# First bias rows copied inside SBUF, and the head of an attention and adapter kernel dealt out anew

## The chip, the cores and the metric

The kernel runs on one core of one Trainium2 chip. The metric is the device time of one execution in microseconds (us). Engines are named PE (matmuls), VectorE or DVE, ScalarE or ACT (exponentials and copies), POOL or GpSimd, and SP, which only issues DMAs here.

## The reference

Attention with eight heads and eight batches over 576 positions of 64 elements, with a bias that depends on the distance of query and key alone, followed by a mixture of low-rank adapters (top two of eight experts) on the joined heads.

```python
scores = scale * np.matmul(q, k.transpose(0, 1, 3, 2))
n = np.abs(pos[:, None] - pos[None, :])
bucket = np.where(n < half, n, large)        # 32 buckets, constant from distance 128 on
scores = scores + bias_table[bucket].transpose(2, 0, 1)[None]
attn = softmax(scores)
x = (attn @ v) joined over heads             # 4608 x 512
logits = x @ w_gate                          # top 2 of 8, softmax over the two
out = x + sum over the two of w * ((x @ A[e]) @ B[e])
```

## The kernel before

Work is cut into 32 units: a unit is a batch `b` and a pair of heads `hp` (four pairs to a batch), so unit u is pair u % 4 of batch u // 4; the text calls units 0 to 5 pairs 0 to 5. In a unit the first 512 positions form the main part, `keys(u, c)` for four key tiles c in the order `KO = (0, 2, 1, 3)`: PE multiplies keys by queries (L434), adds the bias by matmuls of the table `Wt` with a reversed identity `anti` (L439), and ACT takes the exponential into `pk` (L443). The last 64 positions are the tail: `edges(u)` has its scores against the main part (L493, L496, exponential L498 into `pt`), the corners have tail against tail (L470, exponentials L477 or L384 into `pcx`). In edges and corners the bias enters as a factor on the exponentials: `EL`, `ET` and `EC`, applied by `edge_l` (POOL), `edge_t` (DVE) and `corners_bias` (POOL). `step(u, j)` makes half of the unit's values on PE (`values`, L522 to L541) and DVE normalises them.

All orders are written out by hand, and each engine runs its instructions in that order. Queries and keys are loaded in float32 (`load`), cast to bfloat16 (`cast`, `cast_half`), and turned by PE transposes and one DVE copy (`turn`). There are three score tiles in PSUM, taken in rotation by scores and transposes, and two banks named "mm" for values, factors and fillers. `keep_busy` issues filler matmuls. Eight semaphores serve the DMAs in rotation, and a DMA waits until the one before it on its semaphore has landed.

The bias of a head depends on 128 distances. The bias table `btT` (heads in partitions) is spread into a row per head, `gp` (L182 to L196). A row is written to DRAM (`g_d`, L663), and from there `table(h)` reads 64 shifted copies of it, one for each partition, into `Wt` (L208, two DMAs of 224.5 KB, one for each head of the pairs, all four pairs at once). `near_rows` (L204) takes exponentials of parts of `Wt` into `Wn`; `factors_l` (L218) and `factors_t` (L238) turn these on PE and DVE copies them out of PSUM into `EL`, `EC`, `ET`.

Before the loop over u = 2 to 29 stands the head: loads in SP's order, casts dealt to ACT, DVE and POOL, edges of units 0, 1 and 2, corners of batch 0, near rows, the main tiles of units 0 and 1 and one of unit 2, and the two value steps of unit 0. In the loop, a unit's keys stand around the value steps of the unit before.

## Time and profile before

| what | value |
|---|---|
| time, median of 3 runs (lowest, highest) | 193.86 us (193.13, 194.42) |
| the profiled execution's own time | 195.05 us |
| its span | 193.3 us |
| PE busy | 172.6 us (89%) |
| ACT busy | 164.1 us (85%) |
| DVE busy | 136.1 us (70%) |
| POOL busy | 110.5 us (57%) |
| read from and written to HBM | 29.31 MB and 9.45 MB |

The span goes from the first to the last instruction of the profiled execution; its own time has what lies around it too. Busy times are sums over an engine's instructions; a busy matmul is not PE at its peak. A row of groups gives a line, an engine, output and input with shapes, the count, then busy time and mean, then the idle time of the engine just before and what ended it. Times in the text are us from the start of the span.

### The profile page before, as it was taken

What the parts mean: (1) busy time and instruction counts of PE and PEld (TensorE: products, weight loads), DVE (VectorE), ACT (ScalarE), POOL (GpSimd) and SP (SyncE); (2) the same over time, 40 slices, a digit from 0 to 9 for tenths busy, and PEclk for the clock granted to TensorE, in tenths of its full rate; (3) what the DMA queues carried; (4) which work ended last, traced back from release to release, by engine and by line L of the source; (5) the groups of instructions that cost most, each with busy time, mean ns of one, the idle gap of its engine ahead of it and who ended that gap; (6) DMA issues with size and microseconds to landing.
All of it is one profiled execution on the core that took longest, in us unless ns stands there. A gap on an engine that the chain in (4) does not pass through costs nothing.

```text
span 193.3 us, 9928 instructions
## 1 busy us (share of the span) xinstructions
PE 172.6 (89%) x4277; PEld 129.4 (67%) x4299; DVE 136.1 (70%) x345; ACT 164.1 (85%) x199; POOL 110.5 (57%) x249
## 2 busy tenths in 40 slices
...
ACT  3359969999999999999999989999999889898660
...
GB/s 141 241 208 282 237 266 236 215 230 227 197 215 196 222 213 214 206 254 233 249 186 238 213 189 203 257 230 247 216 256 259 197 93 111 83 138 63 3 267 221
DMA packets 63667, 39.40 MB, mean 204 GB/s; under 512 B 17408, under 2 KB 58888, under 8 KB 63624
## 3 DMA queue, kind: packets, MB, share of 16 engines
...
q14 instruction: 10, 0.08, 0.2%
HBM read 29.31 MB, written 9.45 MB: 201 GB/s over the span
## 4 chain that ended last, share of the span: by engine, by line
PE 40%; ACT 33%; issue 10%; DVE 8%; DMA 4%; SPq 0%; ACTq 0%; DVEq 0%
ACT pk L443 26%; PE pv L522 10%; PE tx L379 9%; ACT pt L498 5%; PE sc L496 3%; DMA Wt<-g_d 3%; PE sc L493 3%; PE sc L434 2%; DVE tx L381 2%; PE pv L539 2%; PE pv L530 2%; DMA g_d<-gp 2%; DVE qn L139 1%; PE sc L439 1%; ACT pk L463 1%
## 5 line engine op out<-in xcount | busy, mean ns | idle before, releaser
L443 ACT ACTIVATE pk<-sc 128x1024 bf16<-128x1024 f32 x120 | 113.0, 1037 | 2.4 <-PE sc L439 2.4
L434 PE MATMUL sc<-tx 64*64 64x512 bf16 x480 | 48.2, 384 | 0.2 <-ACT pk L443 0.2
L522 PE MATMUL pv<-v,pk 128*128 128x65 bf16 x992 | 41.4, 193 | 2.9 <-PE sc L439 2.7
L381 DVE COPY tx<-tx 128x2048 bf16<-128x2048 bf16 (+8 forms) x35 | 35.2, 1007 | 11.9 <-PE tx L379 10.0
L439 PE MATMUL sc<-Wt,anti 64*64 64x256 bf16 (+1 forms) x480 | 41.7, 306 | 1.4 <-DMA Wt<-g_d 1.4
L522 PEld LDWEIGHTS <-pk 128*128 128x128 bf16 x1024 | 37.4, 97 | 7.1 <-issue 1.9
L498 ACT ACTIVATE pt<-sc 128x1024 bf16<-128x1024 f32 x32 | 32.8, 1025 | 9.7 <-PE sc L496 7.8
L562 DVE TENSOR_TENSOR xn<-pv,rc 128x320 bf16<-128x320 f32 x62 | 30.5, 492 | 2.1
L503 POOL TENSOR_TENSOR pt<-pt,EL 128x128 bf16<-128x128 bf16 x32 | 13.7, 429 | 31.3 <-ACT pt L498 13.9
L434 PEld LDWEIGHTS <-tx 64*64 64x64 bf16 x480 | 16.9, 105 | 9.9 <-issue 0.7
L561 DVE RECIPROCAL rc<-pv 128x5 f32<-128x5 f32 x62 | 11.9, 191 | 16.1 <-PE pv L569 13.3
L304 DVE TENSOR_TENSOR ot<-dl,xn 128x512 f32<-128x512 f32 x24 | 16.6, 690 | 9.2 <-PE sc L439 6.3
L135 POOL CAST v<-vs 128x512 bf16<-128x512 f32 x32 | 19.8, 621 | 4.0 <-PE pv L541 4.0
L439 PEld LDWEIGHTS <-anti 64*64 64x64 bf16 x480 | 18.2, 105 | 1.9 <-issue 1.7
L139 POOL CAST qn<-qs 128x512 bf16<-128x512 f32 x29 | 18.4, 633 | 0.2 <-DMA qs<-in_q_dram 0.2
L139 POOL CAST kn<-ks 128x512 bf16<-128x512 f32 x29 | 18.0, 620 | 0.0
L539 PE MATMUL pv<-v,pt 128*128 128x65 bf16 x248 | 17.8, 194 | 0.0
L530 PE MATMUL pv<-vb,pt 128*128 128x130 bf16 x124 | 17.4, 223 | 0.0
L379 PEld LDWEIGHTS <-qn 64*128 64x128 bf16 x256 | 7.4, 95 | 13.6 <-issue 5.9
L482 POOL TENSOR_TENSOR pc<-pcx,EC 128x256 bf16<-128x256 bf16 x8 | 5.5, 685 | 18.2 <-ACT pcx L384 15.6
L379 PE MATMUL tx<-ident,qn 64*128 64x64 bf16 x256 | 9.4, 192 | 5.3 <-DVE qn L139 2.8
L539 PEld LDWEIGHTS <-pt 128*128 128x128 bf16 x256 | 14.0, 98 | 0.1
...
## 6 DMA issues: line engine op xcount, KB each, us to landing
...
vs<-in_v_dram SPq DMA_DIRECT2D x64, 128.0 KB, 3.6
ks<-in_k_dram SPq DMA_DIRECT2D x62, 128.0 KB, 4.2
...
vt<-in_v_dram SPq DMA_DIRECT2D x8, 128.0 KB, 4.4
qkt<-in_q_dram SPq DMA_DIRECT2D x7, 128.0 KB, 4.6
qkt<-in_k_dram SPq DMA_DIRECT2D x7, 128.0 KB, 4.8
out_dram<-ot SPq DMA_DIRECT2D x7, 128.0 KB, 2.4
```

The lines of the kernel that those rows point to most:

```text
L135: eng.tensor_copy(t[:, :, :, :D].rearrange("p c h d -> p h c d"), s)
L139: copy(t.rearrange("p c h d -> p h c d"), s)
L379: nc.tensor.transpose(ps[:, a, cols], src(i, a), ident[rows, rows])
L381: copy(sb[:, :n], ps.rearrange("p a (c i) -> p c a i", i=64)[:, :n])
L434: nc.tensor.matmul(sc[prt, h, :], lhsT=kT[rows, c * 128 + f * 64:c * 128 + f * 64 + 64], rhs=qT[rows, :], start=True, stop=False, skip_gro ...
L439: nc.tensor.matmul(_ap(sc[prt, h, :], p0, [[256, 2], [128, 2], [1, n]]), lhsT=turned(h), rhs=_ap(Wt[rows, hp, :], 2 * y0 + (GP if e else 1 ...
L443: nc.scalar.activation(probs[u][0][:, c, :, :], sc, ACT.Exp, scale=scale)
L498: nc.scalar.activation(probs[u][1][:, 64:], sc.rearrange("p h x -> p (h x)"), ACT.Exp, scale=scale)
L522: nc.tensor.matmul(pv[:, o:o + W1], lhsT=pk_slice(u, c, h, j + 2 * f), rhs=vm[:, c, h, :], start=first, stop=False, skip_group_check=True)
L530: nc.tensor.matmul(_ap(pv, h * W1, [[130, 2], [1, W1]]), lhsT=probs[u][1][:, x0:x0 + 128], rhs=tvs[b % 2][:, 2 * hp + h].rearrange("p f d ...
L539: nc.tensor.matmul(pv[:, o:o + W1], lhsT=probs[u][1][:, x0:x0 + 128], rhs=vts[u % NV][:, c, h, :], start=False, stop=False, skip_group_che ...
L562: nc.vector.tensor_tensor(xs[b][:, j, hp], _ap(pv, 0, [[W1, 5], [1, D]]), _ap(rc, 6 * j, [[1, 5], [0, D]]), op=ALU.mult)
```

## The change

The bias table is loaded by two DMAs, one on SP's and one on ACT's queue, so that the first heads of the pairs stand in partitions 0 to 3 and the second heads in 4 to 7. For pairs 0 and 1 four new DMAs on ACT's queue (`table_first`) copy the shifted rows from `gp` straight into `Wt`; `table` brings pairs 2 and 3 by way of `g_d` as before, but is issued behind `vs` and `vt` of unit 0 and `qs` and `ks` of unit 2. Near rows, left and corner factors, top factors and corners are made for pair 0 (corners: pairs 0 and 1) first and for the others later; the later top factors use a score tile and are copied out by ACT. The main tiles of unit 0 follow its edges at once; edges of unit 1 follow these; the first value step of unit 0 stands behind two key tiles of unit 1, the second one behind all four; edges of unit 2 and all its key tiles go into the loop. The casts of units 1 to 3 in the head all go to POOL. Of 24 filler matmuls 18 are left.

```diff
@@ -155,7 +155,8 @@
     GP = 256
     WN = GP + 193
     btT = cp.tile([H, NB], FP32, tag="btT")
-    nc.sync.dma_start(out=btT, in_=bias_table.rearrange("b h -> h b"))
+    for h, eng in enumerate((nc.sync, nc.scalar)):
+        eng.dma_start(out=btT[h * HP:h * HP + HP], in_=bias_table.rearrange("b (g h) -> h g b", h=2)[h])
     load(0, "k", nc.scalar)
     load(0, "q")
     load_tail(0, "qk", 0, 2)
@@ -200,13 +201,21 @@
     EC = cp.tile([128, HP * 64], BF16, tag="EC")
     Wn = cp.tile([128, 2, HP, 68], BF16, tag="Wn")
 
+    def near_one(hp):
+        nc.scalar.activation(Wn[:, :, hp].rearrange("p i (x two) -> p i x two", two=2),
+                             _ap(Wt, 128 + hp * (WN + 1), [[-64, 2], [1, 34], [GP, 2]]), ACT.Exp, scale=scale)
+
     def near_rows(i):
-        nc.scalar.activation(Wn[:, i].rearrange("p g (x two) -> p g x two", two=2),
-                             _ap(Wt, 128 - 64 * i, [[WN + 1, HP], [1, 34], [GP, 2]]), ACT.Exp, scale=scale)
+        nc.scalar.activation(Wn[:, i, 1:].rearrange("p g (x two) -> p g x two", two=2),
+                             _ap(Wt, WN + 129 - 64 * i, [[WN + 1, HP - 1], [1, 34], [GP, 2]]), ACT.Exp, scale=scale)
+
+    def table_first(hp, h, eng):
+        eng.dma_start(out=Wt[h * 64:h * 64 + 64, hp, :WN],
+                      in_=_ap(gp[h * HP + hp:h * HP + hp + 1], 0, [[1, 64], [1, WN]]))
 
     def table(h):
-        nc.sync.dma_start(out=Wt[h * 64:h * 64 + 64, :, :WN],
-                          in_=_dram(gd, 2 * h * GP, [[1, 64], [4 * GP, HP], [1, WN]]))
+        nc.sync.dma_start(out=Wt[h * 64:h * 64 + 64, 2:, :WN],
+                          in_=_dram(gd, (h * HP + 2) * 2 * GP, [[1, 64], [2 * GP, HP - 2], [1, WN]]))
 
     def table_row(rows, hp, y):
         i = 0 if y >= 256 else 1
@@ -215,37 +224,45 @@
     def turned(h):
         return anti[h * 64:h * 64 + 64, 64 - 64 * h:128 - 64 * h]
 
-    def factors_l():
-        n = HP * 64
-        ps = [mp.tile([128, 512], FP32, name="fl", tag="mm") for _ in range(2)]
-        for hp in range(HP):
+    def factor_banks(pool):
+        if pool:
+            t = pool("fl")
+            return [t[:, 0, :], t[:, 1, :]]
+        return [mp.tile([128, 512], FP32, name="fl", tag="mm") for _ in range(2)]
+
+    def factors_l(g0, g1, pool=None):
+        n = (g1 - g0) * 64
+        ps = factor_banks(pool)
+        for hp in range(g0, g1):
+            o = (hp - g0) * 64
             for e in range(2):
                 for h in range(2):
                     rows = slice(h * 64, h * 64 + 64)
                     for f in range(2):
-                        nc.tensor.matmul(ps[h][f * 64:f * 64 + 64, hp * 64 + e * 32:hp * 64 + e * 32 + 32],
+                        nc.tensor.matmul(ps[h][f * 64:f * 64 + 64, o + e * 32:o + e * 32 + 32],
                                          lhsT=table_row(rows, hp, 258 - e),
                                          rhs=_ap(turned(h), f, [[2, 32]]),
-                                         start=(hp == 0 and e == 0), stop=True, skip_group_check=True)
-                    nc.tensor.matmul(_ap(ps[h][rows], n + hp * 64 + e, [[2, 32]]),
+                                         start=(hp == g0 and e == 0), stop=True, skip_group_check=True)
+                    nc.tensor.matmul(_ap(ps[h][rows], n + o + e, [[2, 32]]),
                                      lhsT=table_row(rows, hp, 130 - e), rhs=turned(h)[:, :32],
                                      start=False, stop=True, skip_group_check=True)
         for h in range(2):
             rows = slice(h * 64, h * 64 + 64)
-            nc.vector.tensor_copy(EL[:, :, h, :], ps[h][:, :n].rearrange("p (g x) -> p g x", g=HP))
-            nc.vector.tensor_copy(EC[rows], ps[h][rows, n:])
-
-    def factors_t():
-        ps = [mp.tile([128, 512], FP32, name="ft", tag="mm") for _ in range(2)]
-        for hp in range(HP):
+            nc.vector.tensor_copy(EL[:, g0:g1, h, :], ps[h][:, :n].rearrange("p (g x) -> p g x", g=g1 - g0))
+            nc.vector.tensor_copy(EC[rows, g0 * 64:g1 * 64], ps[h][rows, n:2 * n])
+
+    def factors_t(g0, g1, pool=None, copy=nc.vector.tensor_copy):
+        n = g1 - g0
+        ps = factor_banks(pool)
+        for hp in range(g0, g1):
             for e in range(2):
                 for h in range(2):
                     rows = slice(h * 64, h * 64 + 64)
-                    o = (2 * hp + e) * 64
+                    o = (2 * (hp - g0) + e) * 64
                     nc.tensor.matmul(ps[h][64:, o:o + 64], lhsT=turned(h), rhs=table_row(rows, hp, 258 - e),
-                                     start=(hp == 0 and e == 0), stop=True, skip_group_check=True)
+                                     start=(hp == g0 and e == 0), stop=True, skip_group_check=True)
         for h in range(2):
-            nc.vector.tensor_copy(ET[64:, :, h, :], ps[h][64:].rearrange("p (g x) -> p g x", g=HP))
+            copy(ET[64:, g0:g1, h, :], ps[h][64:, :128 * n].rearrange("p (g x) -> p g x", g=n))
 
     def presets():
         for t in pts:
@@ -361,9 +378,10 @@
         pf = score_tile("tx")
         ps = pf.rearrange("p a x -> p (a x)").bitcast(BF16).rearrange("p (a x) -> p a x", a=2)
         if corner is not None:
-            cs = pf[:, :, 384:]
-            corner_scores(corner, lambda hp: cs[:, hp // 2, (hp % 2) * 64:(hp % 2) * 64 + 64],
-                          lambda hp: hp % 2 == 0)
+            b, g0, g1 = corner
+            cs = pf[:, 0, 384:] if g1 - g0 == 2 else pf[:, :, 384:]
+            corners(b, g0, g1, lambda hp: pf[:, (hp - g0) // 2, 384 + (hp % 2) * 64:448 + (hp % 2) * 64],
+                    lambda hp: hp % 2 == 0)
         sb = txp.tile([128, 16, 2, 64], BF16, name="tx", tag="tx")
         s0 = 0
         for _, k, src, quarter in items:
@@ -380,8 +398,7 @@
             s0 += k
         copy(sb[:, :n], ps.rearrange("p a (c i) -> p c a i", i=64)[:, :n])
         if corner is not None:
-            pxs[corner] = ep.tile([128, HP, 64], BF16, name="pcx", tag="pcx")
-            nc.scalar.activation(pxs[corner].rearrange("p (a g) i -> p a (g i)", a=2), cs, ACT.Exp, scale=scale)
+            corners_exp(b, g0, g1, cs)
         s0 = 0
         for done, k, *_ in items:
             done(sb, s0)
@@ -462,25 +479,33 @@
                                  start=False, stop=True, skip_group_check=True)
         nc.scalar.activation(probs[u][0][:, 2 * j + m, :, :], sc, ACT.Exp, scale=scale)
 
-    def corner_scores(b, place, first):
-        for hp in range(HP):
+    def corners(b, g0, g1, place, first):
+        for hp in range(g0, g1):
             t = tl[(b, hp)]
             for h in range(2):
                 rows = slice(h * 64, h * 64 + 64)
                 nc.tensor.matmul(place(hp)[rows], lhsT=t[rows, 64:], rhs=t[rows, :64], start=first(hp),
                                  stop=True, skip_group_check=True)
 
+    def corners_exp(b, g0, g1, ps):
+        if g0 == 0:
+            pxs[b] = ep.tile([128, HP, 64], BF16, name="pcx", tag="pcx")
+        to = pxs[b][:, g0:g1]
+        if len(ps.shape) == 3:
+            to = to.rearrange("p (a g) i -> p a (g i)", a=ps.shape[1])
+        else:
+            to = to.rearrange("p g i -> p (g i)")
+        nc.scalar.activation(to, ps, ACT.Exp, scale=scale)
+
     def corners_first(b):
-        ps = mp.tile([128, 512], FP32, name="cn", tag="mm")[:, :HP * 64]
-        corner_scores(b, lambda hp: ps[:, hp * 64:hp * 64 + 64], lambda hp: hp == 0)
-        px = ep.tile([128, HP, 64], BF16, name="pcx", tag="pcx")
-        nc.scalar.activation(px.rearrange("p g i -> p (g i)"), ps, ACT.Exp, scale=scale)
-        return px
-
-    def corners_bias(b, px):
+        ps = mp.tile([128, 512], FP32, name="cn", tag="mm")
+        corners(b, 0, 2, lambda hp: ps[:, hp * 64:hp * 64 + 64], lambda hp: hp == 0)
+        corners_exp(b, 0, 2, ps[:, :128])
+
+    def corners_bias(b, g0=0, g1=HP):
         o = 64 * (b % 2)
-        nc.gpsimd.tensor_tensor(pcs[b % 2][:, :, o:o + 64], px, EC.rearrange("p (g i) -> p g i", g=HP),
-                                op=ALU.mult)
+        nc.gpsimd.tensor_tensor(pcs[b % 2][:, g0:g1, o:o + 64], pxs[b][:, g0:g1],
+                                EC.rearrange("p (g i) -> p g i", g=HP)[:, g0:g1], op=ALU.mult)
 
     def edges(u):
         b, hp = units[u]
@@ -656,81 +681,81 @@
         for _ in range(n):
             nc.tensor.matmul(busy, lhsT=zero[:, :128], rhs=zero, start=True, stop=True, skip_group_check=True)
 
+    pxs = {}
     load(1, "qk")
     cast_half(0, "k", 0, nc.scalar)
     cast_half(0, "k", 1, nc.scalar)
-    load(2, "q")
+    for h in range(2):
+        table_first(0, h, nc.scalar)
+    for h in range(2):
+        table_first(1, h, nc.scalar)
     nc.sync.dma_start(out=gd, in_=gp)
+    load(0, "v")
+    load_tail(0, "v")
+    load(2, "qk")
+    for h in range(2):
+        table(h)
+    load_tail(0, "qk", 2)
+    load(1, "v")
+    load(3, "qk")
+    load(2, "v")
+    load(4, "qk")
+    load_tail(1, "qk")
+    load(3, "v")
+    load(5, "qk")
+    load(4, "v")
+    weights_load()
+    load(5, "v")
     cast(0, "q", nc.vector)
     cast_tail(0, "qk", nc.vector, 0, 2)
-    load(2, "k")
-    load_tail(0, "qk", 2)
-    for h in range(2):
-        table(h)
-    load(0, "v")
-    load_tail(0, "v")
-    load(3, "qk")
-    load(1, "v")
-    load(4, "qk")
-    load(2, "v")
-    load(5, "qk")
-    load(3, "v")
-    load_tail(1, "qk")
-    weights_load()
-    load(4, "v")
-    load(5, "v")
     presets()
     cast(1, "q", nc.gpsimd)
-    cast_half(1, "k", 0, nc.scalar)
+    cast(1, "k", nc.gpsimd)
+    cast(0, "v", nc.gpsimd)
     keep_busy(9)
     turn([qk_item(0), tl_item(0, 0, 2)])
     keep_busy(4)
-    cast_half(1, "k", 1, nc.vector)
-    cast_half(2, "k", 0, nc.gpsimd)
-    cast_half(2, "k", 1, nc.gpsimd)
+    for u in range(3):
+        open_probs(u)
+    edges(0)
+    keep_busy(5)
+    near_one(0)
+    keys(0, KO[0])
+    keys(0, KO[1])
+    factors_l(0, 1)
+    edge_l(0)
+    turn([qk_item(1)])
+    keys(0, KO[2])
+    factors_t(0, 1)
+    edge_t(0)
+    keys(0, KO[3])
+    cast_tail(0, "v", nc.gpsimd)
+    corners_first(0)
+    cast(2, "q", nc.gpsimd)
+    corners_bias(0, 0, 1)
+    cast(2, "k", nc.gpsimd)
+    edges(1)
+    for i in range(2):
+        near_rows(i)
+    for c in KO[:2]:
+        keys(1, c)
+    step(0, 0)
+    factors_l(1, HP)
     cast_tail(0, "qk", nc.gpsimd, 2)
+    cast(1, "v", nc.gpsimd)
+    edge_l(1)
+    corners_bias(0, 1, 2)
+    for c in KO[2:]:
+        keys(1, c)
+    turn([qk_item(2), tl_item(0, 2, HP)])
+    step(0, 1)
+    cast(3, "q", nc.gpsimd)
+    cast(3, "k", nc.gpsimd)
+    factors_t(1, HP, score_tile, nc.scalar.copy)
+    edge_t(1)
     nc.gpsimd.memset(sel, 0.0)
     nc.gpsimd.affine_select(out=sel, in_=sel, compare_op=ALU.not_equal, fill=1.0, base=-4,
                             pattern=[[1, 4 + Dm]], channel_multiplier=-4)
-    open_probs(0)
-    open_probs(1)
-    open_probs(2)
-    edges(0)
-    turn([qk_item(1)])
-    keep_busy(4)
-    edges(1)
-    cast(2, "q", nc.vector)
-    keep_busy(5)
-    turn([qk_item(2), tl_item(0, 2, HP)])
-    keep_busy(3)
-    px = corners_first(0)
-    edges(2)
-    near_rows(0)
-    near_rows(1)
-    keys(0, KO[0])
-    keys(0, KO[1])
-    factors_l()
-    keys(0, KO[2])
-    edge_l(0)
-    corners_bias(0, px)
-    cast(0, "v", nc.gpsimd)
-    cast_tail(0, "v", nc.gpsimd)
-    keys(0, KO[3])
-    factors_t()
-    keys(1, KO[0])
-    edge_t(0)
-    keys(1, KO[1])
-    edge_l(1)
-    edge_t(1)
-    cast(3, "q", nc.vector)
-    cast(3, "k", nc.gpsimd)
-    cast(1, "v", nc.gpsimd)
-    keys(1, KO[2])
-    step(0, 0)
-    keys(1, KO[3])
-    keys(2, KO[0])
-    turn([qk_item(3)])
-    step(0, 1)
     cast(2, "v", nc.gpsimd)
 
     tturn = {3 if c == 1 else 6 if c == 2 else 4 * c - 4: c for c in range(1, B)}
@@ -738,8 +763,8 @@
     tq = {w - 1: c for w, c in tturn.items() if c != 2}
     tv = {4 if c == 1 else 6 if c == 2 else 4 * c - 3: c for c in range(1, B)}
 
-    tcorner = {4 if c == 1 else 4 * c - 1: c for c in range(1, B)}
-    pxs = {}
+    tcorner = {4 if c == 1 else 4 * c - 1: (c, 0, HP) for c in range(1, B)}
+    tcorner[2] = 0, 2, HP
 
     def prep(u):
         for x in (u + 2, u + 3)[:1 + (u in wq)]:
@@ -826,12 +851,13 @@
             load_tail(1, "v")
         if u in tload:
             load_tail(tload[u])
-        if u > 2:
-            edges(u)
-        for c in KO[u == 2:2]:
+        edges(u)
+        for c in KO[:2]:
             keys(u, c)
         if u == 4:
             weights_turn(0)
+        if u == 2:
+            turn([qk_item(3)])
         zs = za.pop(u, [None])
         step(u - 1, 0, da.pop(u, []), z=zs[0], zt=ta.pop(u, [None])[0])
         edge_l(u)
@@ -858,7 +884,7 @@
         for bb, i in wq.pop(u, []):
             moe_w(groups[(bb, i)])
         if u in tcorner:
-            corners_bias(tcorner[u], pxs.pop(tcorner[u]))
+            corners_bias(*tcorner[u])
 
     U0, U1, L = NU - 2, NU - 1, B - 1
     act, dve = nc.scalar.copy, nc.vector.tensor_copy
```

## The prediction

> **What bounds the kernel now.** I read the page first, then the instructions of ScalarE in order of time, then the chain of waits and the DMA queue of the first 30 us, where every edit lies.
>
> ```profile
> span 193.3 us, 9928 instructions
> PE 172.6 (89%) x4277; PEld 129.4 (67%) x4299; DVE 136.1 (70%) x345; ACT 164.1 (85%) x199; POOL 110.5 (57%) x249
> ACT  3359969999999999999999989999999889898660
> L443 ACT ACTIVATE pk<-sc 128x1024 bf16<-128x1024 f32 x120 | 113.0, 1037 | 2.4 <-PE sc L439 2.4
> L498 ACT ACTIVATE pt<-sc 128x1024 bf16<-128x1024 f32 x32 | 32.8, 1025 | 9.7 <-PE sc L496 7.8
> ```
>
> The row of tenths shows ACT idle in the first slices, with a dent in the sixth, and near full from there until the last few. The two big exponentials (main scores `pk`, edge scores `pt`) are 145.8 us of its 164.1. The `pk` group waited 2.4 us in all. So ACT sets the pace of the middle, and an exponential that starts earlier in the head should end the kernel earlier by as much. The head:
>
> ```profile
> 0.72 0.96 ACTq L109 DMA_DIRECT2D ks<-in_k_dram  x2
> 4.71 0.40 ACT L651 CAST kn<-ks 128x256 bf16<-128x256 f32 x1 [0.90 <-DMA ks<-in_k_dram]
> 8.06 1.02 ACT L498 ACTIVATE pt<-sc 128x1024 bf16<-128x1024 f32 x1 [0.71 <-PE sc L496]
> 9.82 1.02 ACT L498 ACTIVATE pt<-sc 128x1024 bf16<-128x1024 f32 x1 [0.74 <-PE sc L496]
> 12.57 0.38 ACT L477 ACTIVATE pcx<-cn 128x256 bf16<-128x256 f32 x1 [1.72 <-PE cn L470]
> 13.03 1.02 ACT L498 ACTIVATE pt<-sc 128x1024 bf16<-128x1024 f32 x1
> 14.64 0.82 ACT L204 ACTIVATE Wn<-Wt 128x272 bf16<-128x272 bf16 x2 [0.59 <-DMA Wt<-g_d]
> 15.37 8.32 ACT L443 ACTIVATE pk<-sc 128x1024 bf16<-128x1024 f32 x9
> 25.72 1.02 ACT L443 ACTIVATE pk<-sc 128x1024 bf16<-128x1024 f32 x1 [2.02 <-PE sc L439]
> 27.10 1.94 ACT L443 ACTIVATE pk<-sc 128x1024 bf16<-128x1024 f32 x2 [0.36 <-PE sc L439]
> 29.17 1.02 ACT L498 ACTIVATE pt<-sc 128x1024 bf16<-128x1024 f32 x1
> ```
>
> Columns: start, length, line, operation, and in brackets the idle time and who ended it. From 8.06 (edges of pair 0) to 29.17 (edges of pair 3) ACT worked 1.02 + 1.02 + 0.38 + 1.02 + 0.82 + 8.32 + 1.02 + 1.94 = 15.5 us of 21.1; **5.6 us are holes**. Both `pk` waits of the whole run, 2.02 and 0.36, are among them. Two things make the holes. No `pk` can start before the bias table is in `Wt`, and that takes two hops through DRAM:
>
> ```profile
> 4.91 0.21 DVE gp L195
> 5.31 3.15 DMA g_d<-gp
> 9.11 5.51 DMA Wt<-g_d
> 20.98 2.84 DVE qn L139
> 4.73 0.47 SPq L112 DMA_DIRECT2D qs<-in_q_dram  x1
> 8.48 1.24 SPq L208 DMA_DIRECT2D Wt<-g_d  x2
> DMA to landing us min/median/max: 3.8/4.7/5.5
> ```
>
> The first four are pieces of the chain of waits, then two issues on SP's queue, then the time from issue to landing of the two table transfers: `gp` is done at about 5.3, the table lands at 14.62. The other is one VectorE cast of `qn` that stretched to 2.84 us while POOL was casting too; PE's transposes, and ACT's 2.02 us, waited for it.
>
> **The change, part by part.**
>
> (1) First copies. Four copies (pairs 0 and 1, both heads) go from one row of `gp` straight to 64 rows of `Wt`, issued on ACT's queue behind the two `k` casts. The bias table's own load is split, half of it ahead of ACT's `k` loads. Two issues took 0.96 on that queue, so the casts slip by 0.48: the second ends near 5.6 instead of 5.11, still ahead of its reader, the transposes of `kn` (row below). ACT then issues at 5.6, 6.1, 6.6, 7.1 and is free near 7.6, before its first exponential at 8.06: no cost while an issue takes 0.5 (if each took the 0.6 of a table issue, 0.1 us late).
>
> How long a copy out of one SBUF row takes, the trace does not show. Nearest rows:
>
> ```profile
> ks<-in_k_dram ACTq DMA_DIRECT2D x2, 128.0 KB, 2.7
> Wt<-g_d SPq DMA_DIRECT2D x2, 224.5 KB, 4.7
> 5.86 0.29 PE L379 MATMUL tx<-ident,kn 64*128 64x64 bf16 x8
> 7.70 0.30 PE L496 MATMUL sc<-tx 64*64 64x256 bf16 x4
> 26.46 0.41 PE L434 MATMUL sc<-tx 64*64 64x512 bf16 x4
> 26.83 0.44 PE L434 MATMUL sc<-tx 64*64 64x512 bf16 x4
> ```
>
> From below 2.7 us (same queue, rows in 128 partitions), from above 5.5 (the slower table). I take 3.8, the faster table: same runs of 898 bytes, a quarter of the bytes, but a single source row. Then the copies land at 9.4, 9.9, 10.4, 10.9. PE meanwhile does the edges of pair 0 (its last matmul ends near 8.0) and five filler matmuls, to about 9.2; one set of key matmuls takes 0.37 to 0.5 (26.46 to 26.83, and on to the transposes at 27.32), so pair 0's first scores are there at about 10.2. On ACT: edges 8.06 to 9.08, near rows of pair 0 at 9.9 (half the columns of one of today's two, 0.33 as an estimate from 0.41), first `pk` at **10.25 instead of 15.37**.
>
> (2) The rest of the table still goes through `g_d`, with half the bytes, but is issued later. In the built order SP issues behind the write of `g_d` first `vs` and `vt`, then `qs` and `ks` of pair 2, then the tables; each DMA reuses one of eight semaphores, so `qs` waits for the first copy, the second half of `ks` for the second, the second table for the third.
>
> ```profile
> 12.96 0.98 SPq L109 DMA_DIRECT2D ks<-in_k_dram  x2
> 19.54 1.60 SPq L109 DMA_DIRECT2D vs<-in_v_dram  x2
> ```
>
> With 0.45 for `qs` (its usual 0.47), 0.5 for each half of `ks` (0.98 for two) and 0.6 per table: `qs` 9.4, `ks` 9.85 and 10.35, tables 10.85 and 11.45. Landing after 3.8 (fewer bytes) to 5.5; I take the 4.7 of the middle: **16.15**. ACT has by then done four `pk` (0.92 apart: nine in 8.32) from 10.25 to 13.95, a corner of 0.3 and the edges of pair 1, to 15.2. So a new hole of 0.95 stands before the near rows of the other pairs, which hold up pair 1's `pk` behind them on ACT and, through `Wn`, the remaining factors on PE.
>
> (3) First values, factors, casts.
>
> ```profile
> 24.21 0.67 PE L522 MATMUL pv<-v,pk 128*128 128x65 bf16 x16
> 25.08 0.41 PE L434 MATMUL sc<-tx 64*64 64x512 bf16 x4
> 15.16 0.21 PE L226 MATMUL fl<-anti,Wn 64*64 64x32 bf16 x2
> 15.94 0.40 PE L434 MATMUL sc<-tx 64*64 64x512 bf16 x2
> 18.26 1.31 DVE L248 CAST ET<-ft 64x512 bf16<-64x512 f32 x2
> L139 POOL CAST kn<-ks 128x512 bf16<-128x512 f32 x29 | 18.0, 620 | 0.0
> 10.00:12.00 2.00, 2.00 (x28) 0.78 (x26) 0.60 (x1) 0.84 (x1) 1.50 (x4) 1.00 0.88 220
> 12.00:14.00 2.00, 1.30 (x26) 0.69 (x26) 0.22 (x1) 1.35 (x2) 0.00 (x0) 1.00 1.15 217
> ```
>
> The last two rows are stretches of 2 us: busy times by engine, PE first, then granted clock, DMA share, GB/s.
>
> Near rows end at 16.85, two `pk` of pair 1 run to 18.7. A value step is 0.87 on PE (24.21 to 25.08); the first runs at about 14 to 15 in the hole. The factors of three pairs, three quarters of the 0.8 to 1.0 us that four take, end at 17.55, the third key tile at 18.0: in time. Third and fourth `pk`: to 20.55. The second value step and the last factors on PE lie beside them. Their two copies to `ET` go to ACT instead of VectorE: ACT's 256 columns took 0.38 above, VectorE's pair 1.31, so I put 0.9 for two of 384 columns, between two of 0.38 and 1.31. Edges of pair 2 to 22.4, its four `pk` to 26.1, another 0.3 of corner, PE's edges of pair 3 beside it.
>
> VectorE loses three casts of the head (half of `kn` of pair 1, `qn` of pairs 2 and 3) and with them the 2.84 us; ACT loses one half. POOL takes them, three full casts more at about 0.62 each. Between 8 and 24 it has some 17 operations, about 9 us, the late ones waiting for loads issued behind the tables; casts for pair 4 end near 24.0, their transposes come near 25. Hidden, with 1 us to spare. Fewer fillers on PE (18 for 24) cost nothing: from 12 to 14 it was busy 1.30 of 2.00 and its granted clock stayed at 1.00.
>
> (4) Sum. ACT's work in the stretch rises from 15.5 to 16.6 (ET copies 0.9, a third near-row operation 0.3, a second corner 0.2, less 0.3 for operations that follow each other closely). Holes: 0.8 before the near rows of pair 0, 0.95 before the others, 0.25 elsewhere: 2.0. Edges of pair 3 start at 8.06 + 18.6 = 26.7 instead of 29.17: **2.5 us** less. Behind that the order of the work is today's. The profiled execution took 195.05 us around its 193.3, 1.2 above the median of 193.86. Less 2.5: span 190.8, own time 192.55, median **191.4**. Own bounds from the unknown copy: at 2.7 with tables at 3.8 (near rows at 15.2, no hole there, gain 3.6) 190.2; at 5.5 with tables at 5.5 (copies at 11.1 to 12.6, second table issued at 13.2, landing 18.7, gain 0 within 0.1) 193.9.
>
> A rule of the notes bears on the copy. The Trainium skill, "SBUF — State Buffer", section "Door 1: The DMA port swizzle", has four neighbouring partitions share one port and measured 27.6 GB/s over one. By it, 57 KB out of one row would take 2.1 us beyond any fixed part, as an estimate. No row here has a source of one partition.
>
> **Rivals.**
>
> R1, slower: **one source row serves all 16 DMA engines, and the loads stand behind it.** The four copies are one queue; if each must end before the next moves, they land as far apart as the two tables did today (12.3, which is 8.48 + 3.8, and 14.62: 2.3 apart): 9.4, 11.7, 14.0, 16.3. While an engine waits for its row, what SP queued waits too. `qs`, `ks` and the tables, 0.75 MB, would then move after 16.3 at the 220 GB/s of 10 to 12 us: 3.4 us, and land at about 20.8, 4.65 later than in (2). Gain 2.5 - 4.65 = -2.1: 196.0. It decides for slower from a table landing of 20.5 on (gain -1.9). For it: nothing in the trace shows one row feeding 16 engines. Against: today's table rows overlap in 8 KB of DRAM and still came at 217 GB/s with everything else. The port rule above is this rival's reason. The Trainium skill, "DMA: Bandwidth & Descriptors", section "Issuing engines are not separate DMA queues", adds that both queues run on the same engines; no run here shows what a slow row does to them.
>
> R2, about the same: the port is slow but loads flow beside it. Copies 2.3 apart, second table issued at 14.0, landing 18.7: gain 0, 193.9.
>
> R3, smaller: POOL becomes the bound. Its head has the casts of three engines; if they stretch as VectorE's did, by 2 us, the transposes of pairs 3 and 4 wait 1 us beyond their margin: 192.5 to 193.
>
> R4, the change doesn't do what it says: the loads of pairs 3 to 5, no earlier than today in SP's order, hold the pace; `vs` of pair 3 went out at 19.54 today, and twelve issues of 0.45 to 0.6 behind the tables, from 12.05 on, put it at about 19 again. Then the head's gain is given back by 30 us: 193.4. Against it: the casts of `kn` had no idle time before them (0.0 above), so today's loads are ahead of their readers.
>
> **How the numbers follow.** My forecast 0.50; R1 0.22; R2 0.14; R3 0.08; R4 0.06. A measurement here tells about 1% (1.9 us) from nothing. Faster by over 1% (under 191.9): the forecast and a little of R3, 0.52. Within: 0.26. Slower: R1, 0.22. The forecast's own range is 190.0 to 192.5; the range given reaches to R1's time, 190.0 to 196.0, leaving out a little below and the worse half of R1.
>
> **What would show it.** First `pk` at 10 to 10.5, and the copies on ACT's queue landing within 4 us; near rows of the other pairs at 16 to 16.5; edges of pair 3 near 26.7; no VectorE cast in the head over 1 us; ACT's hole before pair 2's edges under 0.3. If the first copy lands after 11 or the near rows start after 18.5, step (1) or (2) is wrong; if both are right and edges of pair 3 come after 28, step (3); if those are right and the span is not 2 us shorter, the reading that ACT paces the middle is.

## The result, and the profile after

The changed kernel took 194.58 us (median of 20 runs, 192.69 to 196.20) against 193.44 for the kernel before (20 runs, 192.29 to 195.59) in the same comparison: ratio 1.0057, 95% interval 1.0031 to 1.0083. It is slower, by about 1.1 us; the forecast was 2.5 us faster. The profiled execution took 196.05 us, span 194.3, and the one of the kernel before 195.05, span 193.3. Both executions took longer than their kernel's median, by 1.5 and 1.6 us, and that turns out to matter.

From the page of the changed kernel:

```profile
span 194.3 us, 9929 instructions
ACT  3268989999799999996999999999999989898660
L460 ACT ACTIVATE pk<-sc 128x1024 bf16<-128x1024 f32 x120 | 113.1, 1037 | 0.1
L523 ACT ACTIVATE pt<-sc 128x1024 bf16<-128x1024 f32 x32 | 32.8, 1025 | 13.6 <-PE sc L521 7.5
L139 POOL CAST kn<-ks 128x512 bf16<-128x512 f32 x31 | 19.0, 613 | 5.1 <-DMA ks<-in_k_dram 4.6
L139 POOL CAST qn<-qs 128x512 bf16<-128x512 f32 x31 | 19.3, 623 | 3.8 <-DMA qs<-in_q_dram 3.8
```

The main exponentials no longer wait (0.1 us instead of 2.4), but the edge exponentials wait 13.6 us instead of 9.7, and POOL's casts, which stood 0.0 and 0.2 us before (those of `kn` and `qn`), now wait 5.1 and 3.8, for loads. ScalarE's instructions in the head, the answer to the twelve shown of the kernel before:

```profile
5.29 3.70 ACTq L213 DMA_DIRECT2D Wt<-gp  x4
9.04 1.02 ACT L523 ACTIVATE pt<-sc 128x1024 bf16<-128x1024 f32 x1 [3.58 <-issue]
11.78 0.33 ACT L205 ACTIVATE Wn<-Wt 128x136 bf16<-128x136 bf16 x1 [1.72 <-DMA Wt<-gp]
12.14 3.77 ACT L460 ACTIVATE pk<-sc 128x1024 bf16<-128x1024 f32 x4
15.77 0.31 ACT L498 ACTIVATE pcx<-cn 128x128 bf16<-128x128 f32 x1
15.93 1.07 ACT L523 ACTIVATE pt<-sc 128x1024 bf16<-128x1024 f32 x1
17.50 0.69 ACT L209 ACTIVATE Wn<-Wt 128x204 bf16<-128x204 bf16 x2 [0.50 <-DMA Wt<-g_d]
18.09 3.74 ACT L460 ACTIVATE pk<-sc 128x1024 bf16<-128x1024 f32 x4
21.86 0.85 ACT L265 CAST ET<-fl 64x384 bf16<-64x384 f32 x2
22.73 1.02 ACT L523 ACTIVATE pt<-sc 128x1024 bf16<-128x1024 f32 x1
23.65 3.94 ACT L460 ACTIVATE pk<-sc 128x1024 bf16<-128x1024 f32 x4
28.56 1.02 ACT L523 ACTIVATE pt<-sc 128x1024 bf16<-128x1024 f32 x1 [0.40 <-PE sc L521]
```

The first main exponential starts at 12.14 instead of 15.37, and yet the edges of pair 3 come at 28.56, only 0.61 before the 29.17 of the other profile. Issuing the four copies held ScalarE until 9.0, and the first two of them, both heads of pair 0, were waited for until 11.78. On SP's queue, and from the table of DMA issues (the last column is the median from issue to landing):

```profile
10.65 0.37 SPq L112 DMA_DIRECT2D qs<-in_q_dram  x1
12.12 1.24 SPq L217 DMA_DIRECT2D Wt<-g_d  x2
30.31 0.47 SPq L112 DMA_DIRECT2D qs<-in_q_dram  x1
Wt<-gp ACTq DMA_DIRECT2D x4, 56.1 KB, 5.8
```

`qs` of pair 2 went out at 10.65 (4.73 before), the table at 12.12 (8.48), and `qs` of unit 6 at 30.31; the kernel before issued that load at 26.53:

```profile
26.53 0.41 SPq L112 DMA_DIRECT2D qs<-in_q_dram  x1
```

So the loads that units 6 and later need are 3 to 4 us later. What that means in bytes is in the windows of 5 us, the last two columns being the busy share of the 16 DMA engines and GB/s, first the kernel before, then the changed one:

```profile
5.00:10.00 5.00, 4.21 (x70) 2.15 (x71) 3.04 (x8) 1.73 (x4) 2.87 (x10) 1.00 0.79 228
10.00:15.00 5.00, 3.64 (x62) 1.79 (x62) 0.82 (x1) 2.61 (x4) 1.50 (x4) 1.00 1.02 230
15.00:20.00 5.00, 4.07 (x124) 2.38 (x115) 3.54 (x8) 5.00 (x8) 2.53 (x5) 1.00 0.99 277
```

```profile
5.00:10.00 5.00, 3.47 (x44) 1.54 (x46) 1.71 (x5) 1.37 (x2) 2.42 (x9) 1.00 0.88 172
10.00:15.00 5.00, 2.95 (x76) 2.17 (x76) 2.19 (x8) 3.25 (x6) 2.15 (x4) 1.00 0.79 196
15.00:20.00 5.00, 3.77 (x95) 2.19 (x92) 2.27 (x7) 4.50 (x8) 2.10 (x5) 1.00 0.67 182
```

From 5 to 20 us the kernel before moved 5 x (228 + 230 + 277) = 3.68 MB, the changed one 2.75. From 20 to 50 us they move 233 and 238 GB/s in the mean; at that rate the missing 0.93 MB are 3.9 us, as much as the delay seen on SP's queue. But the DMA engines were not full all that time: from 15 to 20 us, when the copies had ended (the last packet of their queue ended at 12.1), their share was 0.67. SP itself had stood still, since a DMA that reuses a semaphore waits for the one before it:

```profile
SPq L112 <- DMA Wt<-gp: 2.0, 1, 2.0
```

Those are 2.0 us ahead of `qs` of pair 2, waited for the first copy. Later one unit shows what it does (POOL's and ScalarE's instructions of the changed kernel):

```profile
46.72 0.61 POOL L139 CAST kn<-ks 128x512 bf16<-128x512 f32 x1 [2.61 <-DMA ks<-in_k_dram]
49.86 1.02 ACT L523 ACTIVATE pt<-sc 128x1024 bf16<-128x1024 f32 x1 [1.08 <-PE sc L521]
```

A cast of `kn` waits 2.61 us for its load, the transposes come late, and the edge exponential of unit 7 starts at 49.86 instead of 49.69: the lead of 0.6 is gone. One more piece of the loss is plain in this trace: at unit 15 PE stood 0.89 us for nothing that the profile's rows name, which no other trace here shows at that place (the last section says what it probably waited for). The end of the span is no part of it: from the edges of unit 31 on, both kernels take 22.7 to 22.9 us.

So the time of an execution is read here in three parts: when the edges of pair 3 start, how long units 3 to 9 and then 3 to 31 take, and the end. All traces of this study, in us:

| trace | first edges | first `pk` | edges of pair 3 | `qs` of unit 6 issued, after the edges of pair 3 by | units 3 to 9 | 3 to 31 | span |
|---|---|---|---|---|---|---|---|
| before | 8.06 | 15.37 | 29.17 | -2.64 | 30.63 | 141.39 | 193.3 |
| e5 (before again) | 9.33 | 16.22 | 28.07 | 0.31 | 30.63 | 141.19 | 192.1 |
| e14 (before again) | 9.33 | 16.51 | 28.35 | -0.63 | 30.63 | 142.77 | 194.0 |
| after | 9.04 | 12.14 | 28.56 | 1.75 | 31.41 | 142.84 | 194.3 |
| e6 (after again) | 9.08 | 11.28 | 27.53 | 1.82 | 30.63 | 140.94 | 191.4 |
| e13 (after again) | 8.91 | 11.46 | 27.57 | 3.33 | 32.16 | 142.80 | 193.2 |
| e1, one pair | 8.21 | 10.57 | 29.36 | 0.14 | 30.63 | 141.44 | 193.5 |
| e2, from DRAM | 9.16 | 11.55 | 27.72 | 2.84 | 32.37 | 142.98 | 193.6 |
| e3, after without v | 8.51 | 11.03 | 27.55 | 1.91 | 30.79 | 141.11 | 191.5 |
| e4, before without v | 9.33 | 16.20 | 28.05 | 0.00 | 30.64 | 140.95 | 192.0 |
| e7, casts on POOL | 8.21 | 16.24 | 28.08 | -0.31 | 30.63 | 141.59 | 192.4 |
| e8, early loads | 9.32 | 11.58 | 27.55 | 1.98 | 31.53 | 142.20 | 192.6 |
| e9, one pair, early table | 8.40 | 10.81 | 26.71 | 1.03 | 30.63 | 140.92 | 190.6 |
| e10, before with late loads | 8.01 | 14.89 | 29.00 | 2.37 | 31.41 | 142.27 | 194.1 |
| e11, table early | 8.52 | 11.54 | 31.47 | -2.32 | 30.63 | 141.53 | 195.8 |
| e12, `ET` on VectorE | 9.16 | 11.61 | 27.15 | 1.74 | 30.93 | 141.22 | 191.4 |
| e15, no copies | 8.03 | 9.72 | 25.32 | 2.08 | 32.33 | 143.06 | 191.3 |
| e16, no copies, no v | 8.41 | 10.10 | 25.38 | 2.19 | 31.10 | 141.40 | 189.7 |

Units 3 to 9 take 30.63 when the loads keep up. In every trace whose load of unit 6 is issued no more than 1.1 us behind the edges of pair 3 they do take 30.63 or 30.64; where it is issued 1.7 to 3.4 us behind, they take up to 1.74 more, in all of these but one (e6). How much more does not follow from the lag alone: 2.08 cost 1.70 in e15, and 3.33 cost 1.53 in e13.

### The profile page after: what moved, and what is told of

It is laid out like the page before. It is cut to its first block, busy times and chain, and to the rows that moved or that the text cites. A ratio compares the mean times of both kernels' runs of the same rounds, so it can differ in the third digit from the quotient of the medians.

```text
span 194.3 us, 9929 instructions
## 1 busy us (share of the span) xinstructions
PE 171.6 (88%) x4270; PEld 129.6 (67%) x4292; DVE 132.1 (68%) x346; ACT 164.7 (85%) x202; POOL 112.0 (58%) x253
## 4 chain that ended last, share of the span: by engine, by line
PE 35%; ACT 32%; DMA 11%; issue 11%; DVE 5%; SPq 1%; POOL 1%; ACTq 0%; POOLq 0%; DVEq 0%
ACT pk L460 26%; PE pv L547 8%; PE tx L397 8%; DMA ks<-in_k_dram 6%; ACT pt L523 4%; DMA Wt<-gp 3%; PE sc L521 3%; PE sc L518 3%; DMA Wt<-g_d 2%; PE pv L564 2%; PE pv L555 2%; DVE tx L399 1%; PE sc L451 1%; ACT pk L480 1%; PE f L903 1%
## 5 line engine op out<-in xcount | busy, mean ns | idle before, releaser
L523 ACT ACTIVATE pt<-sc 128x1024 bf16<-128x1024 f32 x32 | 32.8, 1025 | 13.6 <-PE sc L521 7.5
L456 PE MATMUL sc<-Wt,anti 64*64 64x256 bf16 x480 | 41.8, 306 | 2.0 <-DMA Wt<-gp 2.0
L139 POOL CAST kn<-ks 128x512 bf16<-128x512 f32 x31 | 19.0, 613 | 5.1 <-DMA ks<-in_k_dram 4.6
L139 POOL CAST qn<-qs 128x512 bf16<-128x512 f32 x31 | 19.3, 623 | 3.8 <-DMA qs<-in_q_dram 3.8
L507 POOL TENSOR_TENSOR pc<-pcx,EC 128x256 bf16<-128x256 bf16 (+2 forms) x10 | 5.7, 573 | 15.1 <-ACT pcx L498 15.1
```

What stands on the lines that cost most here:

```text
L139: copy(t.rearrange("p c h d -> p h c d"), s)
L456: nc.tensor.matmul(_ap(sc[prt, h, :], p0, [[256, 2], [128, 2], [1, n]]), lhsT=turned(h), rhs=_ap(Wt[rows, hp, :], 2 * y0 + (GP if e else 1 ...
L523: nc.scalar.activation(probs[u][1][:, 64:], sc.rearrange("p h x -> p (h x)"), ACT.Exp, scale=scale)
```

## The experiments

Ratios are to the kernel before, run in the same comparison. The first four ask whether the one source row is the cause, or the loads.

**e1: only pair 0 copied inside SBUF**, pairs 1 to 3 by way of DRAM.

```diff
-        nc.sync.dma_start(out=Wt[h * 64:h * 64 + 64, 2:, :WN],
-                          in_=_dram(gd, (h * HP + 2) * 2 * GP, [[1, 64], [2 * GP, HP - 2], [1, WN]]))
+        nc.sync.dma_start(out=Wt[h * 64:h * 64 + 64, 1:, :WN],
+                          in_=_dram(gd, (h * HP + 1) * 2 * GP, [[1, 64], [2 * GP, HP - 1], [1, WN]]))
-    for h in range(2):
-        table_first(1, h, nc.scalar)
```

> Changed kernel, but only pair 0 gets its two copies inside SBUF; the table of pairs 1 to 3 comes by way of DRAM. Theory A (a copy out of one SBUF row is slow for all 16 DMA engines, and the loads behind it are what eats the gain): the ACT queue's packets take half of the 41.6 engine-us that they took between 5 and 14 us, qs of pair 2 is issued as before (10.65) or up to 0.5 earlier, tables and later loads 1 to 1.5 us earlier than in the changed kernel, ACT's first edges at 8.1 instead of 9.04, near rows at 16 to 16.5, edges of pair 3 at 27.5; 0.7 to 1.5 us faster than the changed kernel, so ratio to the kernel before 0.998 to 1.002. Rival B (the new dealing of casts, factors and values loses the time, wherever the table comes from): as slow as the changed kernel, 1.005 to 1.007.

194.33 us (12 runs), ratio 1.0035 [0.9991, 1.0079]. Two copies landed in 4.1 us and took ScalarE 1.2 us to issue instead of 3.7, first edges and first `pk` came 0.8 and 1.6 us earlier, the loads kept up. But a hole opened behind:

```profile
20.61 1.94 ACT L460 ACTIVATE pk<-sc 128x1024 bf16<-128x1024 f32 x2 [2.56 <-PE sc L456]
```

The rest of the table now came in time, so there was no wait in which PE could do the first value step; it ran after the first two key tiles of pair 1, the factors behind it waited for its PSUM bank, and the next key tiles behind those. The order suits a hole that this version no longer has.

**e2: the first copies from DRAM**, on SP's queue behind `vs` and `vt` in place of the four on ScalarE's; nothing reads one SBUF row.

```diff
-                      in_=_ap(gp[h * HP + hp:h * HP + hp + 1], 0, [[1, 64], [1, WN]]))
+                      in_=_dram(gd, (h * HP + hp) * 2 * GP, [[1, 64], [1, WN]]))
...
+    for hp in range(2):
+        for h in range(2):
+            table_first(hp, h, nc.sync)
```

> Changed kernel, but the four first copies read the row from DRAM (g_d) and are issued by SP behind vs and vt of unit 0, so that nothing reads one SBUF row 64 times and ACT issues no copies. Theory A: each lands 2.7 to 3.8 us after its issue instead of 5.8, no stretch between 6 and 12 us falls under 150 GB/s, ACT's first edges at 8.06; first pk at 12.3 to 13 as in the changed kernel (12.14), but later loads 1.5 us earlier; ratio to the kernel before 0.993 to 1.000. Rival B: ratio 1.005 or more. Rival C (any small table copy lands late, one row or not): landing 5 us and more, GB/s as low as in the changed kernel.

195.02 us (8 runs), ratio 1.0072 [1.0041, 1.0104]. The row of DMA issues says what a copy of the same size takes out of DRAM:

```profile
Wt<-g_d SPq DMA_DIRECT2D x4, 56.1 KB, 2.7
```

2.7 us, half of the 5.8 out of one row. Yet the kernel is no faster: the first `pk` starts at 11.55, four more issues stand on SP's queue (`qs` of unit 6 at 30.56), and units 3 to 9 lose 1.74. The single row alone isn't the loss.

**e3 and e4: both kernels without the v loads from unit 6 on** (these units use the v of unit 5).

```diff
         for nm in names:
+            if nm == "v" and u > 5:
+                stage[(u, nm)] = stage[(5, nm)]
+                continue
```

> Changed kernel without the loads of vs from unit 6 on (the casts read unit 5's staged tile again), a quarter to a third of the bytes of the middle. To be compared with the kernel before, cut in the same way. Theory A: with loads ahead of their readers again, edges of unit 7 have no hole over 0.4 us (1.08 in the changed kernel) and the head's lead of 0.6 us at the edges of unit 3 stays to the end: 0.3 to 0.9 us faster than its partner. Rival B: 0.5 to 1.5 us slower than its partner, as with all loads.

> Kernel before without the loads of vs from unit 6 on: the partner of the last. Loads do not set its pace (its casts of kn waited 0.0 us), so both theories expect it within 0.3 us of the kernel before; if it is over 1 us faster, loads hold the middle of the kernel before too, and rival R4 of the prediction had more ground than I gave it.

e3: 193.76 us, ratio 1.0028 [0.9995, 1.0060]. e4: 192.79 us, ratio 0.9987 [0.9954, 1.0021]; 12 runs each. With lighter loads units 3 to 9 lose 0.16 in e3's trace. By the ratios the changed kernel is still behind, 1.0028 / 0.9987 or 0.8 us, but the two intervals together are 0.9 us either way. The traces say the opposite (pair 3 at 27.55 in e3 and 28.05 in e4), and each is one execution, e3's 0.5 below its median and e4's 1.0 above. So these two runs do not show how much of the loss lies ahead of the loop. And e4 showed what started the next four: with a head that is the kernel before's, its trace has no 2.02 us hole and pair 3 at 28.05.

**e5 and e6: both kernels once more**, unchanged.

> The kernel before, unchanged: a second trace of its head. Theory H (the trace that the prediction was built on had an unlucky head: the 2.02 us of ScalarE that waited for scores behind the 2.84 us cast of qn on VectorE are no regular part of the kernel, so there was little to gain): no hole over 1 us between the first main exponential (15 to 16.5) and the edges of pair 3, and these start at 27.0 to 28.2. Rival (the hole is regular, and the change gives the gain back later): a cast on VectorE over 2 us again, edges of pair 3 at 28.9 to 29.5.

> The changed kernel, unchanged: a second trace. Theory H: edges of pair 3 at 27.3 to 28.6 again, so 0.5 us around the kernel before and not 2.5 ahead of it; copies out of one row land 5 to 6 us after issue; tables issued at 11.5 to 12.5. The stalls at units 7 (49.9) and 15 (91.2): that of unit 7, a wait for ks, comes back if late loads are its cause (edges of pair 7 over 49.0); that of unit 15, 0.9 us on PE with no cause in the trace, does not (it is chance). Rival (both stalls belong to the change): unit 7 at 49.9 and unit 15 at 91.2 again.

193.92 and 193.19 us for the two profiled executions. The head of e5 on ScalarE, and PE's second block of fillers, with the same row of the prediction's profile behind it:

```profile
9.33 1.02 ACT L498 ACTIVATE pt<-sc 128x1024 bf16<-128x1024 f32 x1 [1.83 <-PE sc L496]
16.22 9.43 ACT L443 ACTIVATE pk<-sc 128x1024 bf16<-128x1024 f32 x10
26.00 1.94 ACT L443 ACTIVATE pk<-sc 128x1024 bf16<-128x1024 f32 x2 [0.35 <-PE sc L439]
28.07 1.02 ACT L498 ACTIVATE pt<-sc 128x1024 bf16<-128x1024 f32 x1
6.71 1.89 PE L657 MATMUL busy<-A 128*128 128x512 bf16 x4
...
6.49 1.04 PE L657 MATMUL busy<-A 128*128 128x512 bf16 x4
```

The hole of 2.02 isn't there: from the first `pk` to the edges of pair 3 it takes 11.85 us, where the prediction's profile took 13.80. It is absent in e4, e14 and e7 too, so of five traces with that order of casts or nearly so, one had it (e10, with its late loads, has two smaller ones, 0.86 and 1.03). This execution was late for another reason, PE at half its pace around 6 to 9 us (below). e6 has pair 3 at 27.53 and loses nothing in the loop, neither at unit 7 nor at unit 15; at 193.19 it is 1.4 under the changed kernel's median.

**e7: the kernel before with the casts of `qn` of pairs 2 and 3 on POOL**, which removes the cause of that hole.

```diff
-    cast(2, "q", nc.vector)
+    cast(2, "q", nc.gpsimd)
-    cast(3, "q", nc.vector)
+    cast(3, "q", nc.gpsimd)
```

> The kernel before with the two casts of qn for pairs 2 and 3 on POOL instead of VectorE, nothing else. It takes away alone what made the 2.02 us hole of the prediction's profile. Theory H (hole rarely there): ratio 0.997 to 1.002, edges of pair 3 at 27.0 to 28.2. Rival (hole in most executions): ratio 0.988 to 0.992, since 2 us of the head are gone.

194.15 us (12 runs), ratio 1.0045 [1.0017, 1.0074]: slower, which neither side expected. On POOL the first of them stands behind other work, and ScalarE's row says what was late next:

```profile
14.14 0.38 ACT L477 ACTIVATE pcx<-cn 128x256 bf16<-128x256 f32 x1 [3.00 <-PE cn L470]
```

The corner of batch 0 came at 14.14 instead of 12.57, the near rows and the first `pk` behind it with it. A hole that opens in few executions isn't worth a permanent 0.9 us (0.45% by the ratio).

**e8: the changed kernel with the loads of pair 2 issued early**, `qs` ahead of the copies, `ks` right behind the write of `g_d`.

```diff
+    load(2, "q")
     for h in range(2):
         table_first(0, h, nc.scalar)
...
     nc.sync.dma_start(out=gd, in_=gp)
+    load(2, "k")
     load(0, "v")
     load_tail(0, "v")
-    load(2, "qk")
```

> The changed kernel with the loads of pair 2 as early as in the kernel before: qs ahead of the copies, ks right behind the write of g_d, so v, tables and all later loads move up by up to 2 us or stay. Theory L (the change is slower because SP issues its loads 3 to 4 us later, and transposes in the loop wait for POOL casts that wait for ks and qs): qs of unit 6 issued by 28.5 instead of 30.3, POOL casts of kn wait under 3 us in all instead of 5.1, and 0.5 to 1.0 us faster than the changed kernel: ratio to the kernel before 0.999 to 1.003. Rival (the order of loads is not it; ScalarE's added work and the copies are): ratio 1.004 to 1.008 and the copies late by as much as the loads are early.

195.53 us (12 runs), ratio 1.0110 [1.0074, 1.0146]: worse than the changed kernel. SP's wait for the copies' semaphores only moved, from `qs` to `vs` of unit 0 (issued at 10.10 instead of 5.64), and everything behind was as late as before: `qs` of unit 6 at 29.53. So it didn't make what it was to test, earlier loads, and tells nothing for or against them.

**e10: the kernel before with late loads**, seven small loads that nobody reads on SP's queue.

```diff
     load_tail(0, "v")
+    late = cp.tile([128, 7, 64], FP32, tag="late")
+    for i in range(7):
+        nc.sync.dma_start(out=late[:, i], in_=q[0, i, :128, :])
     load(3, "qk")
```

> The kernel before with seven small extra loads (32 KB each, into a tile nobody reads) on SP's queue behind vt of unit 0, so that every later load is issued later, qs of unit 6 at 29.5 to 31 instead of 26.5, while the copies, ScalarE's work and the casts stay as before. Theory L (the changed kernel loses in the loop because SP issues its loads 3 to 4 us later): POOL casts of qn and kn wait for DMAs 3 to 9 us in all instead of 0.2, units 5 to 8 lose 0.8 to 1.5 us, ratio 1.003 to 1.008. Rival (SP's lateness is covered): ratio 0.999 to 1.002.

195.76 us (6 runs), ratio 1.0141 [1.0086, 1.0197], more than expected. `qs` of unit 6 went out at 31.37, 4.8 us later than in the prediction's profile, the casts of `qn` waited 2.9 us for loads, and units 3 to 9 lost 0.78; the edges of pair 3 came at 29.00 although the first `pk` had started at 14.89, 2.3 later than that start and e5's 11.85 us to pair 3 would give, so the late loads cost the head as well. Lateness on SP's queue alone, without any of the change, costs more than the change did.

**e11: the changed kernel with the table ahead of `vs` of unit 0**, and `qs` and `ks` of pair 2 ahead of the copies.

```diff
+    nc.sync.dma_start(out=gd, in_=gp)
+    load(2, "qk")
...
-    nc.sync.dma_start(out=gd, in_=gp)
-    load(0, "v")
-    load_tail(0, "v")
-    load(2, "qk")
     for h in range(2):
         table(h)
     load_tail(0, "qk", 2)
+    load(0, "v")
+    load_tail(0, "v")
```

> The changed kernel with SP's order of before as far as possible: g_d, then qs and ks of pair 2, then the rest of the table, and vs and vt of unit 0 behind them (their casts on POOL moved back accordingly). The four copies out of one row stay, and the table still waits for the first copy by its semaphore. Theory L: table issued at 10 to 11 instead of 11.3 to 12.1, qs of unit 6 at 27.5 to 29, no stall at units 5 to 7, edges of pair 3 at 27.0 to 27.8, 0.5 to 1.2 us faster than the changed kernel: ratio 0.997 to 1.002. Rival (copies and ScalarE's added work are the loss): ratio 1.004 to 1.008.

197.58 us (6 runs), ratio 1.0210 [1.0169, 1.0251], far from both. The table came earlier (issued at 10.13, no wait for it any more), and `vs` so late that the first value step waited for its cast, with the next key tiles behind it on PE:

```profile
22.30 1.94 ACT L460 ACTIVATE pk<-sc 128x1024 bf16<-128x1024 f32 x2 [3.51 <-PE sc L456]
```

**e9: the same order with one pair copied**, and the factors moved behind three key tiles of pair 1, ahead of the value step, against e1's hole.

```diff
-    for c in KO[:2]:
+    for c in KO[:3]:
         keys(1, c)
-    step(0, 0)
     factors_l(1, HP)
...
-    for c in KO[2:]:
-        keys(1, c)
+    keys(1, KO[3])
+    step(0, 0)
```

> The same order, but only pair 0 is copied inside SBUF, and the factors of the other pairs stand behind three key tiles of pair 1 and ahead of the first value step, so that PE no longer makes ScalarE wait 2.56 us there as in the version with one pair. Theory L and H together: two copies land by 10.2, first main exponential at 10.6, near rows of the others at 15.3 without a wait for the table, edges of pair 3 at 26.1 to 26.8 against 27.2 in an undisturbed execution of the kernel before, no stall in the loop: ratio 0.994 to 0.999. Rival (copies out of one row hold the loads, however few): qs of unit 6 after 29, ratio over 1.002.

192.93 us (12 runs), ratio 1.0000 [0.9972, 1.0029]. Its trace is nearly what was expected: first `pk` at 10.81, pair 3 at 26.71, loads 1.03 us behind and no stall. That execution was the fastest of its twelve, 0.6 under their median. The loss is gone, and no more than that.

The last five go after what two traces of each kernel left open: 1.1 us between the medians, with pair 3 no later.

**e12: e9 with the copies to `ET` on VectorE** (`factors_t(1, HP, score_tile)` without `nc.scalar.copy`).

> The version with one pair and the early table (median at the kernel before's), with the two copies to ET back on VectorE, so that ScalarE loses 0.85 us of work. Theory H (ScalarE paces the head): edges of pair 3 at 25.9 to 26.3 instead of 26.7, ratio 0.994 to 0.998. Rival (loads and PE hold the pace there, ScalarE's time is not the bound): edges of pair 3 at 26.5 or later, or stalls at units 4 to 8, ratio 0.999 to 1.003.

193.85 us (12 runs), ratio 1.0011 [0.9974, 1.0048]. The edges of pair 3 came at 27.15 in a trace whose first edges were late as well (9.16 for 8.40), so some 0.3 of the 0.85 was kept, and the loads were 1.74 behind with 0.30 lost. An interval this wide allows half a per cent either way; nothing shows a gain.

**e13 and e14: a third trace of each kernel.**

> The changed kernel, unchanged, one more trace. Theory A: edges of pair 3 at 27.5 to 28.6, set by when the copies land (4.5 to 5.8 us after issue). Theory B: at least one stall over 0.5 us at units 5 to 8 with a POOL cast that waits for ks or qs.

> The kernel before, unchanged, one more trace. Theory A: edges of pair 3 at 26.8 to 28.1, with no wait of ScalarE over 1 us after the first main exponential, and a loop of 141.0 to 141.4 from the edges of pair 3 to those of pair 31. Rival: 28.9 to 29.3 with the 2 us wait.

195.00 and 195.80 us. e13 agrees with both theories: the copies landed in 5.2 us, pair 3 at 27.57, loads 3.33 behind, units 3 to 9 losing 1.53, again by transposes that came late, those of unit 6, which PE makes ahead of the edges of unit 5 (the wait named is that of the corner on their copy):

```profile
38.46 0.38 ACT L498 ACTIVATE pcx<-tx 128x256 bf16<-128x256 f32 x1 [1.08 <-DVE tx L399]
```

e14 has no hole either (28.35, again with slow fillers in the head) and loses nothing in units 3 to 9, but its units 3 to 31 took 142.77: PE stood still for 0.43 us at 72.5 and for 1.03 at 149.3, for nothing the profile's rows name. Both sizes were outside what was expected (28.1 at most for pair 3, a loop of 141.4 at most). Such halts occur in both kernels.

**e15: the changed kernel without the four copies**; the rows of pairs 0 and 1 in `Wt` are zeros, so the bias of these pairs is left out.

```diff
-    for h in range(2):
-        table_first(0, h, nc.scalar)
-    for h in range(2):
-        table_first(1, h, nc.scalar)
     turn([qk_item(0), tl_item(0, 0, 2)])
+    nc.vector.memset(Wt[:, :2, :WN], 0.0)
```

> The changed kernel without the four copies: the table rows of pairs 0 and 1 are zeros from a memset, so the bias of these pairs is left out. It takes away the copies, the wait for them and SP's wait for their semaphores. Theory A: near rows of pair 0 follow its edges at 9.2, first main exponential at 9.5 to 9.8, table issued at 9 to 10.5 and landing by 14.5, edges of pair 3 at 25.3 to 26.3, ratio 0.990 to 0.996, so 2 to 3 us faster than the changed kernel: the order of the work would have gained what was forecast, and the copies cost it. Rival (the new order of casts, values and loads costs by itself): edges of pair 3 after 26.8 or stalls in the loop, ratio over 0.999.

192.60 us (12 runs), ratio 0.9943 [0.9918, 0.9968]. The head is the one that was forecast, and better (ScalarE and SP):

```profile
8.95 0.33 ACT L205 ACTIVATE Wn<-Wt 128x136 bf16<-128x136 bf16 x1
9.72 3.77 ACT L460 ACTIVATE pk<-sc 128x1024 bf16<-128x1024 f32 x4 [0.44 <-PE sc L456]
14.41 0.73 ACT L209 ACTIVATE Wn<-Wt 128x204 bf16<-128x204 bf16 x2
25.32 1.02 ACT L523 ACTIVATE pt<-sc 128x1024 bf16<-128x1024 f32 x1 [0.40 <-PE sc L521]
7.21 0.62 SPq L112 DMA_DIRECT2D qs<-in_q_dram  x1
8.95 1.25 SPq L217 DMA_DIRECT2D Wt<-g_d  x2
27.40 0.47 SPq L112 DMA_DIRECT2D qs<-in_q_dram  x1
```

No wait for a copy, none for the table, pair 3 at 25.32. `qs` of pair 2 goes out at 7.21 instead of 10.65, and `qs` of unit 6 at 27.40 instead of 30.31: so some 2.9 of the 3.8 us of lateness came with the copies. Then the earlier head meets the loads, which are still no earlier than before the change (26.53). POOL's casts for unit 6, and the corner behind the transposes that wait for them:

```profile
31.85 0.61 POOL L139 CAST qn<-qs 128x512 bf16<-128x512 f32 x1 [1.79 <-DMA qs<-in_q_dram]
34.03 0.61 POOL L139 CAST kn<-ks 128x512 bf16<-128x512 f32 x1 [1.57 <-DMA ks<-in_k_dram]
36.14 0.38 ACT L498 ACTIVATE pcx<-tx 128x256 bf16<-128x256 f32 x1 [1.01 <-DVE tx L399]
```

Units 3 to 9 give back 1.70.

**e16: e15 without the v loads from unit 6 on**, as in e3 and e4.

> The version without copies (bias of pairs 0 and 1 left out), and without the v loads from unit 6 on (their values are those of unit 5). Theory (the DMA engines, busy at 0.9 to 1.0 from 5 to 45 us, hold units 4 to 9 once the head is earlier): edges of pair 3 at 25.2 to 25.6, units 3 to 9 in 30.6 to 30.9, ratio 0.984 to 0.990, so 1 to 2 us below the version without copies that keeps its v loads. Rival (the early head loses in the loop for another reason, the order of casts or PE): units 3 to 9 over 31.5 again, ratio 0.992 to 0.996.

191.03 us (6 runs), ratio 0.9856 [0.9810, 0.9901]. Units 3 to 9 took 31.10 instead of 32.33. Of the 1.70 that e15 gave back, 0.47 is left; the loads did the rest. That the DMA engines were full, as expected, isn't so in e15's trace: their share is 0.64 to 0.92 in stretches of 5 us from 5 to 45. Whether the bytes or the issues on SP's queue held the units is not told apart.

## Why the prediction was wrong, point by point

**The baseline, step (4): a step that failed.** The sum took 2.5 us off a median, but it was made against a profiled execution whose head was later than usual. The 2.84 us cast and the 2.02 us hole were booked as removed; four other traces that keep the order of before, or nearly all of it, have no such hole, and pair 3 at 28.05 to 28.35 instead of 29.17, three of them with slow fillers. What an execution without hole and with fillers at full pace does can only be put together, since no trace shows one: first `pk` at 14.89 to 15.37 plus the 11.85 of e5 gives pair 3 at 26.7 to 27.2. With the loop of 141 and the end of 22.8, pair 3 at 27.2 is a span of 191.0, or 192.8 us. 13 of the 23 runs of the kernel before beside e7 lie between 192.3 and 192.9, but only 6 of 31 beside e1 and 1 of 23 beside e13. For the median of the main comparison, 193.44, the same sum gives 27.6. e16 against e4, alike in their loads, is 1.8 us between the medians and 2.5 by the ratios; with 25.38 for pair 3 in the one and loops of 141.40 and 140.95, the other's would be at 27.6 to 28.3. The prediction had the warning in its own text (the profiled execution 1.2 over the median) and left the number aside. Against pair 3 at 27.2 to 28.3 the 26.7 that it forecast is a gain of 0.5 to 1.6 us, and not of 2.5.

**The copies, step (1): mis-sized.** 5.3 to 5.8 us to land in the first trace, 4.5 to 5.1 and 5.2 to 5.7 in e6 and e13, not 3.8; above the bound of 5.5 at worst. And issuing was not free: 3.70 us for four on ScalarE's queue, since two of them wait for the semaphores of earlier loads, so the first edges waited 1 us for the engine itself. Near rows of pair 0 at 11.78 instead of 9.9, first `pk` at 12.14 instead of 10.25 (11.28 and 11.46 in e6 and e13). From there to the edges of pair 3 it took 16.4, 16.3 and 16.1 us, where the prediction had 16.45: so the lateness of pair 3 against the forecast, 0.8 to 1.9 us, is that of the first `pk`, 1.0 to 1.9, and nothing behind it. By the prediction's own signs pair 3 after 28 pointed at step (3), and that was not it. The price of the copies on all that follows is the difference of the changed kernel (1.0057) and e15 (0.9943), 1.1% or 2.2 us, with 0.3% either way on each. The order of the work without them did gain, 1.1 us, in a kernel that leaves out the bias of two pairs.

The rule on the port that the prediction cited, the Trainium skill, "SBUF — State Buffer", section "Door 1: The DMA port swizzle", puts rows 0 and 1 of `gp` on one port and 4 and 5 on another, so each port gives two copies here, 115 KB, 4.2 us as an estimate at its 27.6 GB/s, and one in e1, 2.1. Measured, in the middle of each run's copies, are 4.5 to 5.8 for four, 4.1 to 4.4 for two (e1, e9, e12) and 2.7 out of DRAM. The runs have the same order, with a second copy on a port costing less than the estimate's 2.1 (0.1 to 1.7); no run put all copies on one port, so the rule isn't proved by them.

**The loads behind the copies, rival R1: right in kind, smaller than priced.** The page of the changed kernel for 5 to 14 us, by queue (packets, MB, share of the 16 engines' time):

```profile
q1 hardware_dynamic: 2681, 1.40, 55.2%
q10 hardware_dynamic: 320, 0.23, 28.9%
```

The queue with the copies moved 0.23 MB and held the 16 engines for 28.9% of 9 us, 41.6 us of one engine; the other queue took 79.5 us for 1.40 MB, so a third as much for each byte. That and SP's wait for the copies' semaphores (10.65 for `qs`, forecast 9.4) put the table at 12.12 and the near rows at 17.50, forecast 16.15; R1 had the table at 20.8. The time of R1, 196.0, was too far, its sign was right. Its sum doesn't come out either: 16.3 and 3.4 make 19.7, and the text names nothing for the other 1.1. From 19.7 its own working gives a loss of 1.05 and 194.9, near the 194.58 measured, though the copies did not land 2.3 us apart as R1 has it (10.64, 11.69, 12.28).

**Step (3), the casts, held**: no VectorE cast over 1 us, 0.85 for the `ET` copies (0.9 forecast), the second hole 0.50 (0.95). Late was only the `kn` of pair 4, cast until 26.8, 25.7 and 25.6 in the three traces, not 24.0. POOL did not become the bound by its own work (R3); it waits for loads.

**"Behind that the order of the work is today's": the other step that failed**, and rival R4, given 0.06. In the kernel before the DMA engines are 0.79 to 1.02 busy from 5 to 20 us and 0.92 from 20 to 50, so loads lost early are not made up soon, and the casts' idle time of 0.0 was read as ample margin. It was little: in these traces up to 1.1 us of lag behind pair 3 costs nothing, over 1.7 nearly always does. The kernel before had -2.6 to 0.3, the changed one 1.8 to 3.3. An earlier head uses the same margin up as later loads do: in units 3 to 9 e15, with the earlier head, lost 1.70, and e10, with the later loads, 0.78, beside what it lost in the head.

**What the 1.1 us consist of.** By the ratios, one difference after the other: the order of the work alone, with light loads and no copies, is 2.5 us faster (e16 against e4). That this is also the number forecast is luck: the forecast had the copies' waits in it, and a baseline that was late. The full loads take 1.4 of that (1.7 from e16 to e15, of which the kernel before has 0.25), and the copies 2.2 (e15 to the changed kernel). The copies' part is known to about 0.7 us either way, the other two to 1.1 or so; that their sum is 1.1 is no check, since it must be. In the traces the changed kernel loses 0, 0.78 and 1.53 us in units 3 to 9, the kernel before nothing in three. Three traces of each give spans of 191.4 to 194.3 and 192.1 to 194.0, so they don't show the difference of the medians by themselves.
